# Hash attention and an MLP-Mixer block: second-level block products for all channel products, weight pieces on GpSimd, range loads on SyncE

## The chip, the core and the metric

One core of one Trainium2 chip runs the kernel. TensorE multiplies into PSUM, VectorE (DVE) and ScalarE (ACT) read PSUM and work in SBUF, GpSimd (POOL) does a few additions in SBUF and issues some DMAs, SyncE (SP) issues most DMAs. All engines run their instructions in order and wait for one another by semaphores. The metric is device time in microseconds; smaller is better.

## The reference

Attention over 4 batches of 8 heads, 768 positions, head size 64, where a query sees only the keys with the same 6-bit hash; then a Mixer block on the (4, 768, 512) result. All of it is float32.

```python
q_bits = (einsum('bhsd,dk->bhsk', q, proj) > 0)        # and k_bits
mask = q_bucket[:, :, :, None] == k_bucket[:, :, None, :]
attn = softmax(where(mask, q @ k.T / 8, -1e9));  x = attn @ v     # (4, 768, 512)
h = maximum(x.T @ w_tok1, 0) @ w_tok2                  # token mixing, 768 -> 256 -> 768
u = x + h.T
out = u + maximum(u @ w_ch1, 0) @ w_ch2                # channel mixing, 512 -> 1536 -> 512
```

## The kernel before

The program has three stages, one after the other: attention (0 to 310 us), token mixing (310 to 388 us), channel mixing (388 to 789 us). The change is in the third, the function `channels`. It works on columns of `XT`, the 512 channels by 3072 positions, in three ranges of 1024 positions (s = 0, 1, 2). In every range a first product (512 to 1536, with relu) fills the rows `R`, and a second product (1536 to 512) makes the output.

Both products are done as two-by-two block products with seven multiplications instead of eight (p1 to p7, with sums of blocks as operands, in the scheme of Strassen and Winograd). The sums of weights are made once: `SW1` and `SW2` on the first level. On a second level a product p1 to p7 can itself be split by seven; its left operands are then four more sums and three raw quarters of the weight, "pieces", which are made once during the first range and stored in DRAM (`hidden_passed` for the first product, `passed` for the second), and fetched again for every use.

- `hidden(0, t)`, t = 0 to 5, is the first range's first product: one level, seven products of two 512-column matmuls each. Between its own instructions VectorE makes pieces: `jobs` holds lists, and one list is run in the middle of a step and one at its end (lines 818 and 1341). `parts` (line 1046) makes four sums with VectorE and SyncE stores them, from a place that is shared (`seen`) or a free stretch of `area(1)`.
- `hidden_pair(s, t)`, three times in each later range: p2, p6, p3 and p4 are split by seven (`Smaller`, 256 columns), p1, p5 and p7 are whole (512 columns).
- `outputs(s)`, the second product in the order p1, p5, p7, p6, p3, p2, p4: p1 whole (`whole_product`, line 1137), the others split by seven (`product`, line 1151). In the first range p1 reads its weights from `WC2`, where they lie already. Before p5's turn and later, `fetch_left(g)` brings the seven blocks of the product after next into `area(g % 2)`.
- PSUM is used in four pairs of banks, which the products take in turn (`ring`).
- `look()` loads a range of q or k through GpSimd's queue and has ScalarE square it and compare it with a bound (two activations of 128x768, 32 times in all); a flag at the end chooses whether a careful version of the attention has to be run. The calls stand in the later ranges' pairs and in the second products of the first two ranges.

The order of everything is written out by hand: the Python code issues the instructions of all engines in one order, and each engine takes its own in that order. A DMA on SyncE's queue also waits for the DMA eight before it.

Helpers that record many operations have one line in the profile: every channel matmul is L779, copies from PSUM are L785, the piece sums are L1056 to L1059, and their stores L1067 to L1077.

Of the kernel before, what the change touches and what calls it, by code (L numbers as in the profile page):

```python
# [48 lines left out]
def kernel(  # L49
# [701 lines left out]
    def channels(pool, psum, SW1, second, TA, judge):  # L751

        KC, HC, QC = NCB // 2, NHT // 2, NHT // 4
        TB = pool.tile([P, 2, KC, TT], F32, name="TB", tag="TB", bufs=1)
        T = [TA[:, 0], TB[:, 0], TA[:, 1], TB[:, 1]]

        R = [pool.tile([P, 2, HC, TT // 2], F32, name=f"R{i}", tag=f"R{i}", bufs=1) for i in range(4)]
        q1 = pool.tile([P, KC, TT], F32, name="q1", tag="q1", bufs=1)
        last = B * S // (2 * TT) - 1

        def copies():
            return pool.tile([P, 2 * TT], F32, name="c", tag="c", bufs=3)


        ring = [0, 1, 2, 3]

        def bank_pair(i):
            return psum.tile([P, 2, TT], F32, name=f"b{i}", tag=f"b{i}", bufs=1)

        def blocks(n):  # L770

            now = ring[:n]
            ring[:] = ring[n:] + now
            return [bank_pair(i) for i in now]

        def accumulate(ps, left, right, ks, start=True, stop=True):
            ks = list(ks)
            for k in ks:
                nc.tensor.matmul(  # L779
                    ps, left(k), right(k), start=start and k == ks[0], stop=stop and k == ks[-1],  # L780
                    skip_group_check=True,
                )

        def copy(ps, c):
            nc.scalar.copy(c, ps)  # L785
            return c
# [3 lines left out]

        unfinished = []

        def end_rows():

            if unfinished:
                unfinished.pop()()

        def hidden(s, t):
# [6 lines left out]
            ps = [b[:, i] for b in blocks(2) for i in range(2)]  # L805
# [5 lines left out]
            p1 = copy(ps[0], c[0])  # L811
            p5 = copy(ps[2], c[1])
            accumulate(ps[0], lambda k: SW1[:, 0, k, low], lambda k: T[1][:, k], ks, False)
            p7 = copy(ps[3], c[2])
            end_rows()
            nc.vector.tensor_tensor(r[0], split(ps[1]), split(p1), op=ALU.add)
            nc.vector.tensor_scalar(r[0], r[0], 0.0, None, op0=ALU.max)
            for job in jobs.pop(0) if jobs else []:
                job()
            nc.gpsimd.tensor_tensor(p7, p5, p7, op=ALU.add)  # L820
            accumulate(ps[2], lambda k: SW1[:, 2, k, low], lambda k: XT[:, KC + k, sl[1]], ks, False)
            accumulate(ps[3], lambda k: WC1[:, KC + k, high], lambda k: T[3][:, k], ks, False)
            u = copy(ps[0], c[3])
            for k, a in [(3, p7), (1, ps[2]), (2, ps[3])]:
                nc.vector.tensor_tensor(r[k], split(a), split(u), op=ALU.add)
# [325 lines left out]
        def product(s, j, name, q, between, final=None):  # L1151
# [26 lines left out]
            if s < last:  # L1178
                look()
# [294 lines left out]
```

## Time and profile before

| | us |
|---|---|
| median of 3 runs | 796.18 (796.17 to 799.4) |
| the profiled execution | 795.77 |
| its span, first to last instruction | 794.0 |
| TensorE busy in the span | 786.4 |
| channel stage | 388 to 789 |
| `hidden(0, t)`, six steps | 388 to 460 |

A page of the profile is made from one execution. Its rows name engine, line and tile; "busy" is time in instructions, and an engine's idle time is put down to the engine or DMA that ended it. A window's row gives for each engine the busy time and the number of instructions in that stretch, then the granted TensorE clock (1.00 is full), the share of time that the 16 DMA engines were busy, and GB/s. "SPq" rows are SyncE's DMA issues.

### The profile page before, as it was taken

The page shows a single profiled execution, that of the slowest core. Times are in us where ns is not written, and L with a number is a line of the kernel's source. Part 1 is how long each engine was busy: PE and PEld are TensorE (multiplying, and loading weights), DVE is VectorE, ACT ScalarE, POOL GpSimd, SP SyncE. Part 2 cuts the span into 40 slices and gives each one's busy share as a digit, 9 for nine tenths or more (in the row PEclk, how much of TensorE's full clock was granted, in tenths as well). Part 3 has the DMA queues.
Part 4 walks back from the last instruction along what each step waited for, and adds up shares of the span by engine and source line. Part 5 has one row for each costly group of instructions (what it writes and reads, how often), then busy time and mean ns, then how long its engine had stood idle before and what let it go on. Part 6 is the DMA issues. An engine that isn't in the chain of part 4 may idle for free.

```text
span 794.0 us, 12166 instructions
## 1 busy us (share of the span) xinstructions
PE 786.4 (99%) x4661; PEld 464.9 (59%) x4661; DVE 659.7 (83%) x885; ACT 441.4 (56%) x706; POOL 53.5 (7%) x77
## 2 busy tenths in 40 slices
PE   8999999999999999999999999999999999999997
PEld 4444444444444444455544458876667886666886
DVE  5989898988987677999688788988769897778986
ACT  6688888888888886333323221327773335775111
POOL 1000000000000000011121010111110012000001
PEclk9999999999999999999999999999999999999999
DMA  4435353538352425796726994699754578730456
GB/s 163 163 123 163 123 163 123 163 122 246 143 178 87 154 47 166 215 281 173 175 60 228 334 356 145 185 294 283 218 148 139 217 204 195 218 109 1 148 176 159
DMA packets 90974, 138.67 MB, mean 175 GB/s; under 512 B 29656, under 2 KB 63392, under 8 KB 88608
## 3 DMA queue, kind: packets, MB, share of 16 engines
q1 hardware_dynamic: 82752, 112.86, 42.9%
q0 software_dynamic: 7728, 24.64, 14.0%
q8 instruction: 38, 0.62, 0.3%
q10 hardware_dynamic: 432, 0.34, 0.2%
q14 instruction: 24, 0.20, 0.1%
HBM read 97.21 MB, written 33.16 MB: 164 GB/s over the span
## 4 chain that ended last, share of the span: by engine, by line
PE 99%; DMA 1%; SPq 0%; DVE 0%; issue 0%
PE b L779 50%; PE sc L353 20%; PE acc L406 16%; PE t L652 5%; PE t L692 5%; PE sums L430 2%; PE hp L301 1%; DMA qk<-in_qk 1%; PE hw L325 0%; SPq L271 0%; DVE second L1202 0%; PE b L1319 0%; SPq L1469 0%
## 5 line engine op out<-in xcount | busy, mean ns | idle before, releaser
L360 ACT ACTIVATE e<-sc 128x768 f32<-128x768 f32 x192 | 154.1, 811 | 11.6 <-PE sc L353 11.2
L353 PE MATMUL sc<-qk 64*128 64x384 f32 x768 | 152.6, 483 | 0.0
L779 PE MATMUL b<-R,second 128*128 128x256 f32 (+1 forms) x612 | 150.9, 404 | 0.0
L779 PEld LDWEIGHTS b<-R,second 128*128 128x128 f32 x612 | 116.3, 190 | 31.6 <-issue 17.2
L785 ACT COPY c<-b 128x512 f32<-128x512 f32 (+1 forms) x78 | 37.4, 488 | 169.2 <-PE b L779 159.6
L406 PE MATMUL acc<-e,vn 128*32 128x384 f32 x1536 | 127.0, 486 | 0.0
L391 DVE TENSOR_TENSOR esd<-esd,e 128x768 f32<-128x768 f32 x96 | 92.0, 958 | 10.4 <-ACT e L360 0.5
L406 PEld LDWEIGHTS acc<-e,vn 128*32 128x32 f32 x1536 | 49.9, 110 | 73.9 <-issue 73.3
L353 PEld LDWEIGHTS sc<-qk 64*128 64x128 f32 x768 | 68.2, 187 | 40.8 <-issue 35.6
L779 PE MATMUL b<-XT,WC 128*128 128x256 f32 (+1 forms) x264 | 82.5, 456 | 0.0
L779 PEld LDWEIGHTS b<-XT,WC 128*128 128x128 f32 x264 | 50.2, 190 | 29.6 <-issue 25.1
L353 PE MATMUL sc<-bits 64*128 64x384 bf16 x384 | 62.5, 323 | 0.0
L387 DVE SCALAR_TENSOR_TENSOR esd<-e 128x768 f32<-128x768 f32 x32 | 30.6, 955 | 24.5 <-ACT e L360 24.5
L652 PE MATMUL t<-x,W 128*128 128x512 f32 x96 | 41.8, 593 | 0.0
L353 PEld LDWEIGHTS <-bits 64*128 64x128 bf16 x384 | 18.7, 94 | 33.0 <-issue 9.0
L712 POOL DMA_DIRECT2D XT<-second x8 | 9.9, 1232 | 386.0 <-DVE second L711 361.6
L451 ACT COPY rec<-rec 32x384 f32<-32x384 f32 x64 | 32.6, 510 | 5.0 <-DVE rec L445 4.2
L412 ACT ACTIVATE num<-acc,vsum 128x384 f32<-128x384 f32 x32 | 18.6, 581 | 29.8 <-PE acc L406 29.4
L779 PE MATMUL b<-XT,SW 128*128 128x256 f32 (+1 forms) x120 | 34.6, 422 | 0.0
L779 PE MATMUL b<-TA,WC 128*128 128x512 f32 x72 | 33.8, 592 | 0.0
L779 PE MATMUL b<-TA,SW 128*128 128x512 f32 x72 | 32.9, 592 | 0.0
L394 DVE TENSOR_TENSOR esd<-esd,e 128x768 f32<-128x768 f32 x32 | 30.5, 954 | 1.9
(217 smaller groups left out, 1129.3 us busy)
## 6 DMA issues: line engine op xcount, KB each, us to landing
second<-left SPq DMA_DIRECT2D x18, 1344.0 KB
raw<-in_moe_w_ch SPq DMA_DIRECT2D x16, 768.0 KB
qk<-in_qk SPq DMA_DIRECT2D x15, 768.0 KB
seen<-in_qk POOLq DMA_DIRECT2D x21, 384.0 KB, 3.8
WC<-hidden_left SPq DMA_DIRECT2D x15, 448.0 KB
vn<-in_v SPq DMA_DIRECT2D x16, 384.0 KB
vt<-in_vT SPq DMA_DIRECT2D x16, 384.0 KB
x<-bounced SPq DMA_DIRECT2D x4, 1536.0 KB
```

Source lines behind the costliest of these rows:

```text
L353: nc.tensor.matmul(sc[:, i, :HALF], t[rows, 1, P * c : P * c + P], t[rows, 0, qs], start=start, stop=not start,)
L360: nc.scalar.activation(e, sc[:, :, :HALF], ACT.Exp, scale=SCALE)
L387: nc.vector.scalar_tensor_tensor(self.d, es[0], NR * EPS, es[1], op0=ALU.add, op1=ALU.add,)
L391: nc.vector.tensor_tensor(self.d, self.d, e, op=ALU.add)
L394: nc.vector.tensor_tensor(self.d, self.d, self.es[-1], op=ALU.add)
L406: nc.tensor.matmul(acc[D * i + d : D * i + d + 32], vn[:, i, c, d : d + 32], e[:, i], start=(c == 0), stop=(c == NR - 1),)
L412: nc.scalar.activation(nums[self.n][:, self.half], acc, ACT.Identity, scale=-1.0, bias=vsum,)
L451: nc.scalar.copy(rec[other : other + 32, h], rec[at : at + 32, h])
L652: nc.tensor.matmul(ps, W1[:, r, P * j : P * j + P], x[:, r], start=(r == 0), stop=(r == NR - 1),)
L692: nc.tensor.matmul(ps[at], left, right, start=start, stop=True, skip_group_check=True,)
L779: nc.tensor.matmul(ps, left(k), right(k), start=start and k == ks[0], stop=stop and k == ks[-1], skip_group_check=True,)
L785: nc.scalar.copy(c, ps)
```

## The change

Six things change in `channels`:

1. All seven first products of the later ranges, and all seven second products of every range, are split by seven with 256 columns. One routine, `go(y)`, writes the order for both kinds: it interleaves the five multiplications of a product `y` with the last two of the product before it.
2. PSUM is cut into a tile per bank. A product takes two of six banks in turn, `a` and `c`, and a quarter of the last two banks, `b`. The first multiplication's result is copied by ScalarE from `a` to `b` inside PSUM, and further matmuls add to both ("seeded").
3. In the first product the sums over the seven names are run up name after name: VectorE adds the quarters 0 and 1 straight from PSUM, GpSimd the quarters 2 and 3 from SBUF.
4. The pieces of the first weight, now for seven names instead of four, are made by GpSimd, into rows of `R1` to `R3` that are not written yet; those of the second weight, seven instead of six, stay with VectorE. The order of the jobs changes. p1 of the second product no longer reads `WC2` in place: its blocks are stored and fetched like the others (`fetch_left(0)` ahead of the last `hidden` step).
5. `fetch_left` is cut in two, blocks 0 to 4 and the last two. Of the pieces for the next range's first products eight are kept instead of five; in the first range eight fetches are issued together in p2's `work`.
6. `look()` loads by SyncE's queue instead of GpSimd's, and is called in the gaps of second products only (up to three in each), after three loads at the start of `outputs(0)`.

The core of the diff:

```diff
-        ring = [0, 1, 2, 3]
-        def bank_pair(i):
-            return psum.tile([P, 2, TT], F32, name=f"b{i}", tag=f"b{i}", bufs=1)
+        def bank(i):
+            return psum.tile([P, TT], F32, name=f"b{i}", tag=f"b{i}", bufs=1)
...
+        def go(y, work=[], early=[]):
+
+            x, flow.before = flow.before, y
+            y.places()
+            y.mm(y.a, 4, 0)
+            copy(y.b, y.a)
+            y.mm(y.c, 1, 5)
+            y.first_done()
+            if x:
+                x.mm(x.a, 3, 3, False)
+                x.one()
+            run(early)
+            gap(y, 2 if y.patient else 1)
+            y.mm(y.a, 2, 6, False)
+            y.take(y.u, 2)
+            run(work)
+            y.mm(y.b, 5, 2, False)
+            y.second_done()
+            y.zero()
+            gap(y)
+            if x:
+                x.mm(x.c, 6, 7, False)
+                x.two()
+                x.end()
+            y.mm(y.a, 0, 4, False)
+            y.take(y.u5, 3)
+            y.three()
+            y.spent()
+            gap(y)
...
+        class Hidden(Product):
...
+            def head(self, ps, i):
+                if not self.add:
+                    copy(self.sum[0](i), ps)
+                for a, to in zip(self.add, self.sum):
+                    tt(to(i), ps, a(i))
...
+            def end(self):
+                for a, to in zip(self.add, self.sum):
+                    nc.gpsimd.tensor_tensor(
+                        to(slice(2, 4)), split(self.copies[:, 2 * N :]), a(slice(2, 4)), op=ALU.add,
+                    )
+                run(self.after)
+                fetch_hidden_left(self.h + 8)
...
+            plan = dict(
+                p1=([], [e]), p2=([e], [r0]), p6=([e], [u]), p5=([u], [v]), p3=([v], [r1]),
+                p7=([v, u], [r3, w]), p4=([w], [r2]),
+            )
...
-            def parts(w, store, other=False):
+            def parts(w, place, store, engine):
                 def job():
                     (a00, a01), (a10, a11) = weight_quarters(w)
...
+                    engine.tensor_tensor(new[1], a00, a10, op=ALU.subtract)
+                    engine.tensor_tensor(new[0], a10, a11, op=ALU.add)
+                    engine.tensor_tensor(new[2], new[0], a00, op=ALU.subtract)
+                    engine.tensor_tensor(new[3], a01, new[2], op=ALU.subtract)
+                    store(to, [a00, a01, a11])
...
+                return parts(first_weight(name), unwritten(i), store, nc.gpsimd)
...
             return [
-                [], sums, [whole("p1"), second_parts("p7")], *([second_parts(name)] for name in ("p6", "p3", "p5", "p2", "p4")),
-                *([hidden_parts(name)] for name in SMALLER),
+                [hidden_parts("p1", 1), hidden_parts("p2", 2)],
+                [*sums, hidden_parts("p6", 3)],
+                [second_parts("p7"), hidden_parts("p5", 1)],
+                [second_parts("p1", unwritten(0)), hidden_parts("p3", 2)],
+                [second_parts("p6"), hidden_parts("p7", 3)],
+                [second_parts("p3"), hidden_parts("p4", 1)],
+                [second_parts("p5")],
+                [second_parts("p4")],
+                [second_parts("p2")],
             ]
...
+        def fetch_left(g, n=slice(0, 7)):
 
             if g < 7 * (last + 1):
-                name = ORDER[g % 7]
-                n = (HC * 2 if name in WHOLE else 7 * QC) * P
-                nc.sync.dma_start(out=left_at(g)[:, :n], in_=passed[name])
+                sl = slice(QC * P * n.start, QC * P * n.stop)
+                nc.sync.dma_start(out=left_at(g)[:, sl], in_=passed[ORDER[g % 7]][:, sl])
...
+                if s == 0:
+                    work["p2"] += [lambda h=h: fetch_hidden_left(h) for h in range(8)]
...
-                nc.gpsimd.dma_start(out=t, in_=qk[pairs[n][0], pairs[n][1], :, i])
+                nc.sync.dma_start(out=t, in_=qk[pairs[n][0], pairs[n][1], :, i])
...
         for t in range(HC):
             if t == 1:
                 residual(0)
-            if t == 4 if judge else t == 0:
-                if not judge:
-                    fetch_left(0)
+            if t == HC - 2:
                 fetch_left(1)
-            hidden(0, t)
-            for job in jobs.pop(0) if jobs else []:
-                job()
+            if t == HC - 1:
+                fetch_left(0)
+                hidden(0, t, opening(0))
+                break
+            hidden(0, t, jobs.pop(0) if jobs else [])
+            run(jobs.pop(0) if jobs else [])
```

Two classes that `go` is called with are new. `Hidden` is a first product of the later ranges (one matmul for each of its multiplications), `Second` a second product (three matmuls each); `first_done` and `second_done` of `Second` make the operand sums that were made in `product`, `spent` and `end` issue the two parts of `fetch_left(g + 2)`. In `hidden` the addition into `r[3]` moves behind the other additions of the step.

## The prediction

> **What bounds the kernel now.** I read the page first, then the chain of waits, then the timelines of the engines in the stage that the change rebuilds (388 to 789 us). The page says that TensorE never rests:
>
> ```profile
> span 794.0 us, 12166 instructions
> PE 786.4 (99%) x4661; PEld 464.9 (59%) x4661; DVE 659.7 (83%) x885; ACT 441.4 (56%) x706; POOL 53.5 (7%) x77
> PEclk9999999999999999999999999999999999999999
> ```
>
> The chain that ended last is TensorE almost alone. Its pieces give the price of a pass (start, us, what; each f32 product of the code is two passes):
>
> ```profile
> 350.54 9.03 PE t L692 x28
> 359.57 10.30 PE t L652 x24
> 388.17 364.23 PE b L779 x1308
> 752.51 36.28 PE b L779 x168
> ```
>
> L652 passes are 512 columns wide: 10.30/24 = 0.429 us. The last 168 passes are 256 wide: 36.28/168 = 0.216 us. So a pass costs its columns, halves are not dearer, and the only gains left are fewer columns. Anything that makes TensorE wait is a loss, since today nothing does.
>
> The first range's `hidden` steps (t = 0 to 5, 28 passes or 12.07 us each, 388.1 to 460.5) share their time with the making and storing of weight pieces. There the DMA engines are already full (columns: window, us, busy time and count of each engine, granted clock, DMA share, GB/s):
>
> ```profile
> 437.80:446.00 8.20, 8.20 (x21) 3.65 (x20) 5.85 (x12) 3.05 (x6) 1.27 (x1) 1.00 1.00 337
> 446.00:456.00 10.00, 10.00 (x25) 4.50 (x24) 7.00 (x14) 1.67 (x4) 0.00 (x0) 1.00 1.01 328
> 456.00:466.00 10.00, 10.00 (x24) 4.38 (x24) 8.85 (x17) 3.13 (x6) 1.91 (x2) 1.00 0.94 367
> ```
>
> And VectorE and GpSimd hinder each other there. Two timelines of that stage, VectorE's and GpSimd's (start, us, engine, line):
>
> ```profile
> 407.93 1.76 DVE L746 TENSOR_TENSOR second<-second 128x1536 f32<-128x1536 f32 x1
> 409.72 2.70 DVE L747 TENSOR_TENSOR second<-second,second 128x1536 f32<-128x1536 f32 x1
> 420.64 1.52 DVE L1059 TENSOR_TENSOR seen<-second,seen 128x384 f32<-128x384 f32 x1
> 425.53 0.56 DVE L1056 TENSOR_TENSOR seen<-second 128x384 f32<-128x384 f32 x1 [2.31 <-DMA left<-seen]
> ```
>
> ```profile
> 408.24 2.57 POOL L820 TENSOR_TENSOR c<-c 128x512 f32<-128x512 f32 x1 [6.79 <-ACT c L785]
> 420.26 1.48 POOL L820 TENSOR_TENSOR c<-c 128x512 f32<-128x512 f32 x1 [9.45 <-ACT c L785]
> 456.31 1.27 POOL L820 TENSOR_TENSOR c<-c 128x512 f32<-128x512 f32 x1 [10.74 <-ACT c L785]
> ```
>
> At 456 GpSimd's add met no VectorE work and took 1.27 us. At 408 it met L746 and took 2.57; L747, queued behind it, took 2.70 instead of 1.76. At 420 L1059 took 1.52 instead of 0.56. So VectorE instructions with two SBUF inputs and GpSimd's adds run one after the other. The fourth row shows the other chain: the next piece waits 2.31 us until the store of the last one has left the shared place.
>
> **TensorE's gain.** In the two later ranges p1, p5 and p7 of the first product go from 4 products of 512 columns (8 passes, 3.43 us) to 7 of 256 (14 passes, 3.02 us): 0.41 us, times 3 names, 3 pairs, 2 ranges = 7.3 us. The second product's p1 goes from 24 passes of 512 (10.29 us) to 42 of 256 (9.07 us): 1.22 us, three times, 3.7 us. Sum 11.0 us. With no new wait the profiled execution (795.8 us, of which 794.0 are span) would become 784.8, the median 796.2 becomes 785.2.
>
> **The new wait before the second product.** Until now p1 took its weights from `WC2` in place. Now it needs its seven blocks by `fetch_left(0)`, which SyncE issues only after every piece of both weights was made and stored, since it overwrites the tile that p2's last blocks are stored from. p1 cannot start before that fetch lands; today it starts at 460.5. Two sums say when:
>
> By bytes: SyncE's queue carries 7 first and 7 second names of 1344 KB (1.376 MB) each, 19.3 MB, the residual of 4 times 512 KB, 2.1 MB, and both fetches, 2.75 MB: 24.1 MB. Before, up to the same point, it was less, and no fetch was awaited at 460. The first piece can leave when GpSimd has made four, about 405. At the 328 to 367 GB/s of the full windows that takes 66 to 74 us: 471 to 479, and about 1 to 2 us to land. A wait of 11 to 20 us.
>
> By engines: GpSimd gets 28 pieces of 384 columns. No row has one; by the 1.27 us of 512 columns one costs 0.95 (bounds: 0.56, VectorE's own, and 1.27). With five adds of 1.27 that is 33 us. VectorE's two-input work up to p2's pieces is 4 x 1.76 (sums), 28 x 0.56 (pieces), about 10 x 0.69 and 10 x 0.42: 34 us. If they alternate, 67 us from 399.7 end at 467, and waits for the shared place (2.3 us as in the row above, six of them, partly beside GpSimd's turn) take it to about 472. Then p2's blocks must be stored (six DMAs, 1.376 MB, 4.1 us at 337 GB/s, and issue and landing 2.5) and p1's fetched (4.1 and 1.5): about 484. If VectorE and GpSimd did not hinder each other this sum falls below the other one, and bytes decide.
>
> I take 484, a wait of 23 us, with 11 and 30 as ends. On GpSimd the add for `p7` of the next t is queued behind up to twelve pieces, on VectorE `r[3]` waits for that add and the next pieces stand behind `r[3]`; on SyncE the first range loads and the next fetch stand behind `fetch_left(0)`. Within the 23 us TensorE also waits earlier (t = 2 on: a copy needs a buffer that GpSimd's add still reads), which is the same time, not more.
>
> **The second products of the first range.** 20 range loads (393 KB) now fall in these seven products, on SyncE's queue, in order with the weights. DMA time by rows: a fetch of 1.376 MB at 138 GB/s and share 0.39 (730 to 740 us) is 3.9 us, six of them 23; range loads at that rate 1.1 each, 22; eight accumulating output stores at 162 GB/s and share 0.89 (388 to 392) 2.9 each, 23; eight pieces for the next range at 315 GB/s and share 1.10 (530 to 536) 1.6 each, 13. That is 81 us in 63.5 us of TensorE. What is not needed at once slides into the next stage. But p4's blocks 3 and 6 and three range loads are queued behind the eight pieces, and ScalarE, waiting for a range, holds up copies that free banks. Ends: 0 (all of it slides) and 17.5 (nothing does). I take 4, nearer to nothing, because the stage after has room (shares about 0.5 to 0.9).
>
> The Trainium skill ("DMA: Bandwidth & Descriptors", Queues, rings and completion order) says that each DMA engine takes turns between the queues that have work. That speaks against the move of the range loads: on GpSimd's queue they had a turn of their own, on SyncE's they stand behind the weights. In this trace GpSimd's range loads landed 3.8 to 6.1 us after issue; no row here has one on SyncE's queue. By the rule alone a load behind the eight pieces would wait their whole 13 us (an estimate), where ScalarE comes for it a product, 9 us, later: the sum would be 4 us longer.
>
> **Parts near nothing.** The seed: a ScalarE copy from PSUM to PSUM, not in the trace; nearest is 0.37 us for 128x256 from PSUM to SBUF. TensorE does two other products between (0.86 us in the first product, 2.6 in the second). Cover is gone if a relu of 0.58 stands ahead: 0.1 us, up to 36 times, 3.6 us at most; taken as 0. GpSimd's adds in the first product, 1.27 us once or twice per 3.02 us, meet VectorE instructions that read PSUM, which no row shows hindered: 0. A tile per bank frees banks earlier, but TensorE waits for none: 0, no gain. The end has one VectorE add fewer after the last pass: -0.4 us.
>
> Sum: 796.2 - 11.0 + 23 + 4 = 812 us.
>
> **Rivals.**
> Covers hold (faster): stores run at the best rate seen for 4 us (409 GB/s, 456 to 460), so 24.1 MB take 59 us, p1 waits about 5 us, and nothing else shows: 785 to 792. It decides if p1's fetch lands before 471.5, when the wait eats the 11 us. Against it: the full windows above, in which less was stored. 0.16.
> Only bytes decide: wait 11 to 20, later stage 0 to 4: 796 to 808. For it: pieces on GpSimd leave VectorE 16 instructions fewer. 0.24.
> Both chains, my forecast: wait 20 to 30, later 0 to 8: 805 to 822. 0.46.
> The first range's second products become DMA-bound as well: 10 to 17 more on 23: 818 to 832. 0.14.
>
> Half a per cent, 4 us, is about what can be told from no change. Below 792.2 lies the first rival, 0.16; between 792.2 and 800.2 a third of the second, 0.08; above it 0.76. The range 791 to 828 leaves out most of the first rival and the top of the last.
>
> **What would show it.** Right: 14 passes per 3.02 us in all first products of the later ranges; rows of 384 columns on VectorE in the `hidden` steps stretched to about 1.5 us beside GpSimd; TensorE idle for 20 us or more before the first 256-wide pass, released by the DMA that fills `second`. Wrong: p1 starting by 465, GpSimd's pieces ending by 435, or a DMA rate over 400 GB/s throughout. If TensorE stands in the second products for ScalarE, the third term is larger.

## The result and the profile after

The changed kernel takes 877.63 us (median of 4 runs, 874.0 to 882.8) against 797.79 us of the kernel before: 1.100 times as long, interval 1.094 to 1.107. The prediction was 812, range 791 to 828: the direction was right, the size far off. The profiled execution took 874.0 us, its span 872.2.

The head of the changed kernel's page:

```profile
span 872.2 us, 12935 instructions
PE 795.1 (91%) x4823; PEld 499.1 (57%) x4823; DVE 646.1 (74%) x936; ACT 460.0 (53%) x830; POOL 141.1 (16%) x126
PEclk9999999999999999999998799789999996999999
```

TensorE, which never rested, is idle for 9% of the span. Two things more: it is busy 8.7 us longer than before although its passes are 11 us shorter, and its clock is no longer full in five of the 40 slices. TensorE's timeline gives the places (start, us, instruction; in brackets the idle time before it and what ended that):

```profile
485.24 2.93 PE L777 MATMUL b<-R,second 128*128 128x256 f32 x6 [14.06 <-DMA second<-left]
561.90 2.93 PE L777 MATMUL b<-R,second 128*128 128x256 f32 x6 [12.74 <-ACT c L783]
568.65 1.22 PE L777 MATMUL b<-WC 128*128 128x256 f32 x2 [3.81 <-ACT b L783]
...
734.88 1.22 PE L777 MATMUL b<-WC 128*128 128x256 f32 x2 [15.06 <-ACT c L783]
...
852.05 1.56 PE L777 MATMUL b<-second,second 128*128 128x256 f32 x6 [2.37 <-DVE second L787]
854.91 9.45 PE L777 MATMUL b<-R,second 128*128 128x256 f32 x42 [1.29 <-DVE c L787]
```

The first row is the wait that was predicted, at 485 instead of 484. The others were not predicted, or only as a few microseconds. The six passes in the first row hold TensorE for 2.72 us, to the next start at 487.96, where six take 1.30 at full speed: each of the long waits (3.8 us and more here) is followed by slow passes.

To compare runs I use a **loss** for each stage: the time from its first pass to the first pass of the next stage, less its passes. H0 is `hidden` of the first range (72.1 us, as before), O0, O1, O2 are the second products (7 x 9.07 = 63.5), H1 and H2 the later first products (21 x 3.02 = 63.4). Where `go` interleaves, the last multiplications of a stage stand behind the first ones of the next: 2.6 us move from O0 and O1 into the stage behind, 0.9 from H1 and H2. The passes sum to 389.4 us against the measured 400.8 of the kernel before. Losses, in us, and the time of each experiment's one run:

| run | H0 | O0 | H1 | O1 | H2 | O2 | time |
|---|---|---|---|---|---|---|---|
| changed kernel | 23.2 | 2.0 | 26.8 | 4.2 | 20.1 | 8.8 | 874.0 |
| e1 pieces on VectorE | 17.1 | 2.7 | 31.2 | 4.2 | 19.8 | 9.0 | 871.0 |
| e9 residual later | 19.1 | 2.0 | 23.9 | 4.2 | 18.5 | 9.4 | 864.7 |
| e15 both of these | 13.5 | 1.5 | 26.6 | 4.2 | 19.8 | 9.4 | 864.7 |
| e7 p1 in place | 8.1 | 11.2 | 26.0 | 4.2 | 19.1 | 9.1 | 866.4 |
| e2 range loads on GpSimd | 24.5 | 3.1 | 30.4 | 5.0 | 20.3 | 9.5 | 880.0 |
| e3 fetches spread | 23.0 | 4.5 | 25.1 | 4.2 | 19.8 | 9.6 | 872.6 |
| e10 no late range loads | 22.7 | 1.8 | 27.2 | 4.5 | 21.6 | 9.1 | 875.5 |
| e13 half the range check | 23.3 | 1.5 | 26.7 | 4.2 | 21.9 | 9.1 | 875.0 |
| e4 adds on VectorE | 23.0 | 2.8 | 23.1 | 3.2 | 12.4 | 8.8 | 861.2 |
| e5 four stores | 22.8 | 8.7 | 15.4 | 8.8 | 6.2 | 10.3 | 858.7 |
| e6 = e4 + e5 | 22.9 | 8.0 | 17.2 | 8.0 | 7.0 | 10.4 | 857.1 |
| e14 = e6 + half the range check | 23.0 | 5.2 | 5.6 | 8.0 | 5.6 | 10.4 | 843.7 |
| e8 = e6 + e7 | 8.9 | 9.7 | 18.4 | 6.3 | 5.6 | 10.4 | 844.6 |
| e11 all remedies | 2.2 | 13.1 | 4.5 | 8.8 | 7.3 | 12.3 | 834.4 |

For the changed kernel: 795.8 (profiled before) - 11.4 (passes) + 85.1 (losses) + 2.6 (from the last pass to the end: 7.8 instead of 5.2) + 1.9 (the channel stage began later, at 389.9) = 874.0. Such a start varies from 387.4 to 390.3 over the runs, and four runs of the changed kernel spread over 9 us, so the losses, not the times, carry the small differences. Each of these is one run too: in the runs whose edit leaves a stage alone H0 lies between 22.7 and 24.5 and H2 between 18.5 and 21.9, and differences of that size say nothing. The kernel before took 795.7 to 798.5 beside the experiments.

**What stands behind the loss in H2.** The change doubles the accumulating stores of the output: each of the sums that were added up in SBUF before is now sent out by itself. From the lists of DMA issues, the kernel before and then the changed one (count, size, median us to landing):

```profile
out<-second POOLq DMA_DIRECT2D x10, 512.0 KB, 8.4
```

```profile
out<-second POOLq DMA_DIRECT2D x17, 512.0 KB, 8.3
out<-q POOLq DMA_DIRECT2D x4, 512.0 KB, 8.2
```

21 stores instead of 10. GpSimd's timeline of the changed kernel at the end of the second range:

```profile
700.55 1.22 POOL L1296 DMA_DIRECT2D out<-second  x1 [5.04 <-issue]
706.89 1.21 POOL L1296 DMA_DIRECT2D out<-second  x1 [5.11 <-issue]
716.79 1.22 POOL L1296 DMA_DIRECT2D out<-second  x1 [8.69 <-ACT c L783]
725.01 1.21 POOL L1296 DMA_DIRECT2D out<-q  x1 [6.99 <-issue]
731.39 1.22 POOL L1296 DMA_DIRECT2D out<-second  x1 [5.17 <-issue]
732.15 1.76 POOL L1035 TENSOR_TENSOR R<-c,second 128x512 f32<-128x512 f32 x1
```

A store is busy for 1.2 us, but the next starts 6.3 to 9.9 us after it, in three of the four gaps for nothing that the profile names ("issue"). The landings show what it is: the stores at 694.30, 700.55, 706.89, 716.79 and 725.01 land after 5.9, 6.0, 9.6, 7.9 and 6.1 us, and the next store starts 0.3 us after each landing. In all 17 traces of this case no accumulating DMA on this queue starts before the one ahead of it has landed (0.26 us after it at the least). Other instructions don't wait so: the add at 732.15 starts 0.76 us behind the last store, and in the kernel before a plain range load does the same:

```profile
539.26 1.24 POOL L1222 DMA_DIRECT2D out<-second  x1 [10.78 <-DVE XT L848]
540.03 1.07 POOL L1307 DMA_DIRECT2D looked<-in_qk  x1
```

So a store does not fill the queue by itself; it is the next store that waits, and all that stands behind that one. Four are still to come when the third range begins at 706, and the first `L1035` add of that stage stands behind all of them. ScalarE waits for this add with its relu, and for a range load one range earlier:

```profile
559.69 0.84 ACT L1388 ACTIVATE looked<-looked 128x768 f32<-128x768 f32 x1 [13.57 <-DMA looked<-in_qk]
...
733.94 0.63 ACT L793 ACTIVATE R<-R 128x512 f32<-128x512 f32 x1 [15.74 <-POOL R L1035]
```

Behind both stand copies that free TensorE's banks. The range load comes late because SyncE, whose DMAs each wait for the eighth before them, was held up by the fetches ahead of it:

```profile
538.93 12.10 SPq L975 DMA_DIRECT2D SW<-hidden_left  x5
551.45 3.72 SPq L1399 DMA_DIRECT2D looked<-in_qk  x1
```

**Short waits in H1 and H2.** Some 4 us of the loss in each of these two stages have another cause. Where nothing long stands in the way, seven first products (98 passes, 7 x 3.02 = 21.1 us) take 22.56 us, at full clock and with the DMA engines nearly idle; the kernel before took 22.39 us for the same seven (windows of the changed kernel and of the kernel before, columns as in the prediction):

```profile
766.29:788.85 22.56, 22.13 (x100) 18.20 (x99) 12.53 (x30) 11.23 (x30) 8.85 (x8) 1.00 0.14 41
```

```profile
524.80:547.19 22.39, 22.39 (x82) 15.20 (x81) 17.95 (x29) 11.49 (x20) 4.74 (x6) 1.00 0.98 265
```

The 1.4 us are three waits of 0.24 us and one of 0.69 in every group of seven. Each stands where ScalarE does a relu (L793) right ahead of the copy that TensorE needs. No run here moves these relus, so that this cause is read from the rows alone. Two of the waits in the changed kernel, ScalarE's rows and then TensorE's:

```profile
618.06 0.63 ACT L793 ACTIVATE R<-R 128x512 f32<-128x512 f32 x1
618.59 0.38 ACT L783 COPY b<-b 128x256 f32<-128x256 f32 x1
620.07 0.63 ACT L793 ACTIVATE R<-R 128x512 f32<-128x512 f32 x1 [1.10 <-POOL R L1035]
620.60 0.35 ACT L783 COPY c<-b 128x256 f32<-128x256 f32 x1
```

```profile
619.02 0.70 PE L777 MATMUL b<-WC,SW 128*128 128x256 f32 x2
621.01 0.70 PE L777 MATMUL b<-WC,SW 128*128 128x256 f32 x2 [0.43 <-ACT c L783]
```

### The profile page after: what moved, and what is told of

It reads as the page before. It is cut to its first block, busy times and chain, and to the rows that moved or that the text cites. A ratio compares the mean times of both kernels' runs of the same rounds, so it can differ in the third digit from the quotient of the medians.

```text
span 872.2 us, 12935 instructions
## 1 busy us (share of the span) xinstructions
PE 795.1 (91%) x4823; PEld 499.1 (57%) x4823; DVE 646.1 (74%) x936; ACT 460.0 (53%) x830; POOL 141.1 (16%) x126
## 3 DMA queue, kind: packets, MB, share of 16 engines
q0 software_dynamic: 8160, 17.83, 12.4%
## 5 line engine op out<-in xcount | busy, mean ns | idle before, releaser
L777 PE MATMUL b<-R,second 128*128 128x256 f32 x594 | 140.2, 388 | 29.7 <-DMA second<-left 14.1
L783 ACT COPY c<-b 128x256 f32<-128x256 f32 (+1 forms) x146 | 58.5, 405 | 130.5 <-PE b L777 107.0
L391 DVE TENSOR_TENSOR esd<-esd,e 128x768 f32<-128x768 f32 x96 | 92.0, 958 | 10.4 <-ACT e L360 0.5
L793 ACT ACTIVATE R<-R 128x512 f32<-128x512 f32 x48 | 29.7, 630 | 59.8 <-POOL R L1035 28.5
L777 PE MATMUL b<-XT,SW 128*128 128x256 f32 (+1 forms) x208 | 60.7, 405 | 0.0
L777 PE MATMUL b<-XT,WC 128*128 128x256 f32 (+1 forms) x164 | 54.9, 453 | 0.0
L787 DVE TENSOR_TENSOR R<-R 128x768 f32<-128x768 f32 x45 | 44.5, 1000 | 6.5 <-PE b L777 5.9
L787 DVE TENSOR_TENSOR c<-b,c 128x256 f32<-128x256 f32 x72 | 29.7, 421 | 26.2 <-ACT c L783 21.7
L777 PEld LDWEIGHTS b<-XT,SW 128*128 128x128 f32 x208 | 39.0, 190 | 11.7 <-issue 5.5
L1035 POOL TENSOR_TENSOR R<-c,second 128x512 f32<-128x512 f32 x24 | 31.4, 1309 | 65.7 <-DVE c L787 65.4
```

Source lines behind the costliest of these rows:

```text
L391: nc.vector.tensor_tensor(self.d, self.d, e, op=ALU.add)
L777: nc.tensor.matmul(ps, left(k), right(k), start=start and k == ks[0], stop=k == ks[-1], skip_group_check=True,)
L783: nc.scalar.copy(to, ps)
L787: nc.vector.tensor_tensor(to, a, b, op=op)
L793: return lambda: nc.scalar.activation(a, a, ACT.Relu)
L1035: nc.gpsimd.tensor_tensor(to(slice(2, 4)), split(self.copies[:, 2 * N :]), a(slice(2, 4)), op=ALU.add,)
```

## The experiments

### The wait before the second product (H0)

**e1**

```diff
-                return parts(first_weight(name), unwritten(i), store, nc.gpsimd)
+                return parts(first_weight(name), unwritten(i), store, nc.vector)
```

> The first weight's pieces are made by VectorE instead of GpSimd; nothing else differs from the changed kernel. Question: what holds the second product's p1 until 485 us. Theory 'DMA': the 24.1 MB of stores and fetches decide, GpSimd's pieces were over by 443.7 and the DMA engines ran at share 1.0 and 351 to 385 GB/s from 428 to 460, so the first 256-wide pass of the second product starts at 480 to 488 again and the time stays within 4 us of 874. Rival 'engines' (the sum that the prediction took): VectorE and GpSimd hold each other up, without that p1 starts at 470 to 478 and 8 to 15 us are saved. Third: VectorE's own queue gets 28 pieces of about 0.56 us (16 us) more and becomes later itself, p1 at 490 or more.

Measured: p1 at 477.2, 89.2 us after the first layer's first pass instead of 95.3. So the engines hold each other up by 6 us, less than the rival said (477.2 lies in its stretch only because the stage began 1.9 us earlier in this run), and DMA alone is not it either. H1 lost 4.4 us more in this one run.

**e9**

```diff
             if t == 1:
-                residual(0)
...
             if t == HC - 1:
                 fetch_left(0)
+                residual(0)
```

> The four stores of the residual of the first range (2.1 MB), which SyncE issues in the changed kernel after the first step, are issued after the fetch for p1; nothing else differs. If DMA bytes alone hold p1 until 485, it starts 5 to 6 us earlier relative to the first pass of the first layer (2.1 MB at 351 to 385 GB/s; 95.3 us from there in the changed kernel, so 89 to 91). If the chain of VectorE, GpSimd and the shared place decides, it starts where it did (95 to 96). With both, in turn, something between, 91 to 94. The whole time gains no more than that, and gives back some of it where the 2.1 MB then run.

Measured: 91.2 us instead of 95.3, in the stretch named for "both, in turn".

**e15**, both edits.

> First weight's pieces on VectorE and the residual's four stores after the fetch for p1, each of which alone took 6.1 and 4.1 us from the first layer's first range (95.3 us; 72.1 without a wait). If the two are links of one chain in turn (first engines, then bytes), they add: 84 to 86 us. If bytes alone are left once the engines are out of the way, the residual's 2.1 MB give their full 6 us: 82 to 84. If they cover each other: 88 to 89.

Measured: 85.6 us. They add up: first a chain of engines, then bytes. The windows of the changed kernel show the two parts (window, us, busy of PE, PEld, DVE, ACT, POOL, clock, DMA share, GB/s):

```profile
410.00:420.00 10.00, 10.00 (x25) 4.41 (x24) 9.90 (x7) 2.44 (x5) 9.76 (x6) 1.00 0.40 152
430.00:440.00 10.00, 10.00 (x24) 4.39 (x24) 9.39 (x11) 1.17 (x2) 9.75 (x8) 1.00 1.05 379
450.00:460.00 10.00, 5.59 (x13) 2.20 (x12) 4.20 (x9) 0.59 (x1) 1.27 (x1) 1.00 1.04 379
```

At 410 VectorE and GpSimd are full and the DMA engines wait for them; from 430 on the DMA engines are full, and at 450 VectorE is not.

**e7**

```diff
+            if s == 0 and judge:
+                for i in range(KC):
+                    ps = flow.bank()
+                    accumulate(ps, lambda k: second["WC2"][:, k, P * i : P * i + P], lambda k: R[0][:, :, k], range(HC))
...
+                    copy(q1[:, i], ps)
...
+                fetch_left(2)
```

> In the first range alone the second product's p1 takes its weights from WC2 in place, 24 passes of 512 columns (10.3 us instead of 9.1), as the kernel before does; its fetch there is left out, the rest is the changed kernel. Theory 'two separate waits': the wait before the second product (24.7 us and 2 to 3 of slower clock) goes, 1.2 comes back, 850 us. Rival 'one backlog': what is left out is 1.4 MB of some 24; the stores and loads that were worked off in these 25 us now lie beside the second products, and ScalarE and TensorE wait there or at the head of the next stage instead: of the 25 us at least 12 return, 861 to 875 in all. I hold the rival for the likelier, since the DMA engines ran at share 1.0 from 428 to 470 and from 508 to 570.

Measured: 866.4 us, within the rival's stretch. The long wait is gone, but of the 25.2 us lost in H0 and O0 only 5.9 are gained, with p1's 1.2 us of longer passes already taken out: 8.1 us remain in H0, mostly waits of 1.5 to 2.8 us for copies and rows (e11, with pieces on VectorE, has 2.2), and O0 loses 11.2 where it lost 2.0. The stores and loads that were worked off during the wait now lie beside the second products: TensorE waits 5.53 us for weight blocks at 491.77.

### The second range's start (O0 and H1)

**e2**, the range loads back on GpSimd's queue.

```diff
-                nc.sync.dma_start(out=t, in_=qk[pairs[n][0], pairs[n][1], :, i])
+                nc.gpsimd.dma_start(out=t, in_=qk[pairs[n][0], pairs[n][1], :, i])
```

> The range loads go back to GpSimd's queue. Question: the first stage of the second range lasts 92.0 us (548.1 to 640.2) instead of 63.5. Theory 'queue': its waits of 13.6 us of ScalarE for 'looked' and 4.6 for 'seen', which hold up the copies that free banks, come from the range loads' place behind the eight weight fetches on SyncE's queue; on GpSimd's queue they land before they are wanted and the stage takes 68 to 78 us, 14 to 24 less. But GpSimd's queue then has 20 loads more ahead of its adds, so its adds may cost up to 5 back. Rival 'bytes': the DMA engines have 81 us of work for 63.5 us of TensorE there, whichever queue it stands in: the stage stays above 85 us.

Measured: O0 and H1 lose 33.5 instead of 28.8, and the second range's first stage takes 95.6 us, above 85, as the rival said. Yet it is again a place in a queue: ScalarE now waited 20.0 us for the load at 555.86, which stands 0.71 us behind an output store on GpSimd's queue, and that store had to wait for the landing of the one before.

**e3**

```diff
-                    work["p2"] += [lambda h=h: fetch_hidden_left(h) for h in range(8)]
+                    for j, name in enumerate(ORDER[:6]):
+                        work[name] += [lambda h=h: fetch_hidden_left(h) for h in ([0, 1] if j == 0 else [6, 7] if j == 5 else [j + 1])]
```

> The eight weight fetches for the second range, which were all issued within the second product p2, are spread over p1 to p2 (two, one, one, one, one, two), in the same queue; the bytes are the same. Theory 'queue': no range load then stands behind eight fetches; ScalarE's wait of 13.6 us and TensorE's of 12.7 us at 560 go, the stage of the second range takes 66 to 75 us instead of 92.0, 17 to 26 less in the whole. Rival 'bytes': the waits only move forward, into the second products p5 to p3 of the first range, and the time from 485 to 640 stays within 6 us of the changed kernel's 155.

Measured: as the rival said. O0 and H1 lose 29.6, and from 482.6 to 638.3 it is 155.7 us. The 12.7 us wait became one of 5.3 us for a copy and one of 9.8 us behind GpSimd's add.

**e10**

```diff
-            elif flow.looks and y.patient:
+            elif flow.looks and y.patient and y.g not in (5, 6):
```

> In the first range's p2 and p4 no range load is issued or taken up; these few come in the second range's products instead. All else as in the changed kernel. Theory: ScalarE's wait for 'looked' (13.6 us at 560), with TensorE's 12.7 us behind it, is the wait for one range load behind eight weight fetches; here there is no such load, so that wait goes, but what was queued with it stays: p4's last two blocks (384 KB) stand behind the same eight fetches, and TensorE then waits 4 to 8 us for them ('DMA second<-left'): the time from the first pass of the second product (485) to that of the second range's outputs (642) falls from 157 to 145 to 151. Rival: the DMA engines decide, not the order: the wait for p4's blocks is as long as the one for ScalarE, 155 to 158 as before.

Measured: the wait for a range load is gone, TensorE waits 7.8 us for p4's blocks as expected ('DMA second<-left', at 555.9), but the stage is not shorter: 11.9 us behind GpSimd's add follow at 582.7. O0 and H1 lose 29.0, and from 484.4 to 639.5 it is 155.1 us: the theory's sign, and the rival's number.

**e13**, no range load in the first range after the first three; half of the check is left out.

```diff
-            elif flow.looks and y.patient:
+            elif flow.looks and y.patient and y.g > 6:
...
-        unseen = [(n, i) for n in range(len(pairs)) for i in range(2)] if judge else []
+        unseen = [(n, i) for n in range(len(pairs)) for i in range(2)][:16] if judge else []
```

> Left out: half of the range check, 16 of 32 loads, namely those that stand in the first range's second products after the first three (some 18 of 393 KB, 7 MB there); the second range keeps its 13 or so. All else as in the changed kernel. In the changed kernel the loss over passes is 2.0 us in the first range's second products and 26.8 in the second range's first products. Theory 'bytes': 7 MB at 330 GB/s are 21 us of full DMA engines; without them what is left fits, the two losses together fall from 28.8 to 5 to 12. Rival 'GpSimd's store queue': eight stores, 6.2 to 10 us apart, still reach 30 us into the next stage, GpSimd's adds stand behind them, and the two losses stay at 18 to 27, with ScalarE waiting for GpSimd's add (R<-...L1035) in the place of the range load, as in the third range.

Measured: 28.2 instead of 28.8, although 20 loads (7.9 MB) are gone from this stretch; four of them now come a range later. TensorE's timeline, and ScalarE's:

```profile
551.77 2.90 PE L777 MATMUL b<-R,second 128*128 128x256 f32 x6 [5.16 <-DMA second<-left]
580.04 1.22 PE L777 MATMUL b<-WC,SW 128*128 128x256 f32 x2 [12.29 <-ACT c L783]
```

```profile
579.10 0.63 ACT L793 ACTIVATE R<-R 128x512 f32<-128x512 f32 x1 [12.97 <-POOL R L1035]
```

The rival's sign is there, and its 18 to 27 us were still too few: with the range loads away, GpSimd's add behind the stores ends the wait, as in H2, 34.5 us after the stage's start, where the add's last wait ended 37.3 us after it in the changed kernel.

### GpSimd's stores and adds (H1 and H2)

**e4**

```diff
-                    nc.gpsimd.tensor_tensor(
+                    nc.vector.tensor_tensor(
                         to(slice(2, 4)), split(self.copies[:, 2 * N :]), a(slice(2, 4)), op=ALU.add,
```

> The adds that end a product of the first layer go from GpSimd to VectorE. Theory 'queue': on GpSimd they stand behind output stores whose issue takes 5 to 7 us each, so that ScalarE waited 15.7 us for one of them and TensorE 15.1 us behind it at 734; without that the stage of the third range takes 63 to 68 us instead of 85.3, that of the second range 2 to 6 less than 92.0, in all 19 to 28 us less. Rival 'DMA': the output stores and weight fetches are late by themselves, TensorE waits then for a DMA in the same place, and less than 6 us are saved. Against both: VectorE gets up to 36 adds of 256 to 512 columns (0.4 to 0.7 us, 14 to 25 us in two stages of 63.5) and could become late: then its waits show on ScalarE and TensorE as DVE.

Measured: H2 loses 12.4 instead of 20.1, H1 23.1 instead of 26.8; 12.8 us in the whole, between the theories. VectorE does not become late by its adds. It waits for the stores themselves, which still read the places that the stage writes its sums to:

```profile
729.17 0.42 DVE L787 TENSOR_TENSOR second<-b,second 128x256 f32<-128x256 f32 x1 [7.50 <-DMA out<-second]
```

**e5**, four stores per range. The sums are made in SBUF, p2 and p4 add in place, and the places are renamed so that the one stored last is needed last.

```diff
-            e, u, v, w = map(place, (3, 0, 1, 2))
+            e, u, v, w = map(place, (3, 2, 1, 0))
...
-            sums = [add(q7, q7, q6), add(q5, q5, q6)]
-            sums += [store(q5, 0, 1), *([store(q7, 1, 0), store(q7, 1, 1)] if more else [store(q6, 1, 1)])]
+            sums = [add(q7, q7, q6), add(q6, q6, q5), add(q5, q5, q7), store(q5, 1, 1)]
...
-                final = None
+                final = True if name in ("p2", "p4") else None
```

> Each range's output goes out in 4 accumulating stores instead of 8 (2 instead of 5 in the last range, whose DMA for the residual becomes an add): the quarters are summed on VectorE first, two adds of 1024 columns (1.22 us) more per range, and p2 and p4 add in place, 8 copies per range moving from ScalarE to VectorE. Theory 'GpSimd's issue': in the changed kernel stores that stand one behind the other on GpSimd start 6.2 to 6.4 us apart (725.01 and 731.39; 851.54, 857.82 and 864.00), whatever the DMA engines do, so six stores from the middle of a range's second products on take 37 us and reach 25 us into the next stage, where GpSimd's adds stand behind them and VectorE waits for places that they still read. With 4 stores the third range's first stage falls from 85.3 to 64 to 70 us, the second range's from 92.0 to 76 to 86 (the range loads' wait stays), the end loses 4 to 8: 834 to 850 in all. Rival 'the adds': GpSimd's adds are late by themselves, beside VectorE; then the third range's stage stays above 80.

Measured: in H2 ScalarE waits 1.1 us at most for GpSimd's add, and TensorE behind it 0.43; H2 loses 6.2 instead of 20.1, H1 15.4 instead of 26.8. The stores start up to 11.5 us apart beside other DMA work, not 6.2 to 6.4 "whatever the DMA engines do". The whole is 858.7, above the stretch that I gave: the sums make VectorE late (waits of 3.0 us in O0 and 2.6 in O1, with slow passes behind both), so that O0 and O1 lose 8.7 and 8.8 instead of 2.0 and 4.2, and the end gains only 1.3 in all.

**e6**, e4 and e5 together.

> Four stores per range, and the adds that end a first product on VectorE. If the stores are the cause of both waits in the third range's first stage (GpSimd's adds behind them, VectorE's wait for places that they read), this stage is within 2 us of 63.5 now, and the whole is 2 to 8 us below the kernel with four stores alone. Rival 'VectorE': 17 us more of adds there make VectorE late, and this is no better than four stores alone.

Measured: 857.1; H2 loses 7.0, not under 2, and the whole is only 1.6 us less, which is the rival's number. With H2 at 12.4 by e4 alone, 6.2 by e5 alone and 7.0 by both, the adds' place no longer matters once the stores are few: the two remedies remove one cause. Of what stays, some 4 us are the short waits.

**e14**, e6 and e13 together.

> Left out: the same half of the range check, on top of four stores per range and VectorE's adds at the end of a first product. Both theories expect most of the two losses (25.2 us with the four stores and VectorE's adds) to go: to 8 to 13, about the 15.0 that the same two stages lose one range later, where there are few range loads. If they stay above 18, neither bytes of range loads nor stores are the cause, and the eight weight fetches themselves are.

Measured: O0 and H1 lose 10.8, within 8 to 13. So H1 had two chains side by side, each about as long as the other: range loads and blocks behind the weight fetches on SyncE's queue, and the adds behind the stores on GpSimd's. Away with the first alone (e13): 0.6 us. With the second alone (e6): 3.6. With both: 18.0. The 3.6 are net of 6.0 us that the sums on VectorE cost in O0; by H1 alone it is 0.1, 9.6 and 21.2, still far more together than one by one. Whether the bytes of the range loads or their place in the queue make the first chain is not shown: e13 and e14 take away both.

### All together, and the clock

**e8**, e6 and e7.

> The three edits together: four stores per range, the adds on VectorE, p1 of the first range in place. If the three causes are separate their gains add up: the kernel with the first two, less 24 us, about 805 to 815. If there is one backlog of DMA work in the first range, fewer stores (2 MB of the output, each read and written) shrink it too, and waits of 10 to 25 us stay between 500 and 590, released by DMA or by ScalarE's range loads: 815 to 835.

Measured: 844.6, above both stretches: p1 in place gains 12.6 us here.

**e11**: e1, e4, e7, e5 with two of its sums on GpSimd, no range load in p2 and p4 of the first range (e10), and the eight fetches from p5 to p4.

> All remedies in one kernel: first weight's pieces, and the adds that end a first product, on VectorE; four accumulating stores per range, two of their sums on GpSimd itself; p1 of the first range in place; the eight fetches one or two to a product from p5 to p4; no range load in p2 and p4 of the first range. From 844.6 us of the three remedies before: about 6 less by the pieces (waits of 1.5, 2.1 and 2.8 us at 444 to 458), 8 to 12 less at 548 to 560 (6.7 and 4.1 us of waits and the slower clock after them), 4 to 7 less by VectorE's waits of 2.3 to 3.8 us at the sums: 818 to 828. If the DMA engines simply have too much to do between 420 and 570, the waits at 548 return as single waits for weight blocks in p7 to p3, and it stays above 832. Below the kernel before (796) it does not get by either theory.

Measured: 834.4, above 832 as the second theory said, but without its sign: no wait for weight blocks is longer than 0.6 us (at 513). H0 has nearly no loss (2.2), and of the 4.5 in H1 most are the short waits, since seven first products still take 22.38 us. What is left elsewhere are waits of 1 to 3 us for VectorE's sums, and what follows them, which neither theory had. TensorE's timeline at the opening of the second range's second product, and windows of the same place (columns as above; the clock is the third number from the right):

```profile
613.23 2.31 PE L777 MATMUL b<-q,second 128*128 128x256 f32 x6 [2.16 <-DVE q L787]
615.33 2.41 PE L777 MATMUL b<-R,second 128*128 128x256 f32 x6
```

```profile
612.00:614.00 2.00, 0.77 (x3) 0.72 (x4) 1.97 (x4) 0.00 (x0) 0.00 (x0) 0.96 0.00 0
614.00:616.00 2.00, 2.00 (x6) 1.59 (x5) 2.00 (x4) 0.37 (x1) 0.00 (x0) 0.50 0.00 0
616.00:618.00 2.00, 2.00 (x7) 1.64 (x7) 2.00 (x4) 0.22 (x2) 0.00 (x0) 0.69 0.00 0
618.00:620.00 2.00, 2.00 (x11) 1.76 (x10) 1.97 (x3) 1.97 (x5) 0.00 (x0) 1.00 0.00 0
```

A wait of 2.2 us, and then about 3.4 us at half clock (0.2 + 2.0 + 1.2 from the three clocks below 1), so that twelve passes from 613.23 take 4.35 us to 617.58 instead of 2.59.

**e12** asks whether the wait alone does this, in the kernel before.

```diff
+            for _ in range({1: 7, 2: 11}.get(t, 0)):
+                copy(ps[0], c[3])
             p1 = copy(ps[0], c[0])
```

> The kernel before, with two waits put into it where nothing else is short: ScalarE copies one PSUM bank 7 times more in the first layer's second step and 11 times more in its third, ahead of the copy that frees that bank for TensorE; the extra copies go to a buffer that is overwritten later. A copy takes about 0.52 us and there are 2.65 us of cover, so TensorE waits 1.0 to 1.5 us in the second step (about 407) and 3.0 to 3.7 us in the third (about 420). Question: does a wait cost more than itself? Theory 'clock': after a wait of over 2 us TensorE's granted clock is 0.50 for some 3 us (in the kernel with all remedies a wait of 2.16 us at 613 was followed by six passes in 2.31 and six in 2.41 us instead of 1.3), after one of 1.8 us or less it is not: so after the first wait passes keep 0.43 us each, after the second 5 to 8 of them take 0.86, and the third step costs 2 to 3 us more than its wait; in all 5.5 to 8.5 us over the kernel before if nothing else covers them. Rival: the lower clock comes with something else that those places share (the change from one stage to the next, full DMA engines); here, with DMA share 0.5 to 0.8, both steps cost their waits alone, 4 to 5 us.

Measured, on TensorE's timeline:

```profile
408.93 1.98 PE L779 MATMUL b<-TB,SW 128*128 128x512 f32 x4 [1.43 <-ACT c L785]
...
425.11 2.94 PE L779 MATMUL b<-TB,SW 128*128 128x512 f32 x4 [3.90 <-ACT c L785]
427.84 2.66 PE L779 MATMUL b<-XT,SW 128*128 128x512 f32 x4
430.34 1.88 PE L779 MATMUL b<-TB,WC 128*128 128x512 f32 x4
```

After 1.4 us the next group starts 1.82 us later (1.72 without a wait); after 3.9 us the next two start 2.73 and 2.50 us later: 1.8 us more than the wait. In all 803.5 against 795.7, and 7.8 us of span, of which the starts show 7.4: 1.6 and 4.1 by the waits (the groups ahead start at 405.62 and 419.33) and 1.8 by the clock. The clock follows the wait, with no change of stage near it.

How long must a wait be? In the changed kernel 1.79 us at 645, 2.13 at 452 and 2.37 at 852 left the clock at 1.00, 2.91 at 461 and all longer ones did not; in e11 2.16 us was enough, in e6 1.98 (706.86), while in e4 3.29 (838.49) was not. The Trainium skill ("TensorE: Matmul & The Clock Gate", Part 1) tells of a freely running window of about 3.4 us: an idle window halves the clock, a busy one restores it. The 3.4 us at half clock agree, and so does the grid: in the changed kernel the granted clock falls at 461.87, 475.52, 554.03 and 724.70, whole multiples of 3.413 us apart. Such a window would explain why waits of like length end differently. That only gaps over 3.4 us do harm, as its rule has it, the waits at 461 and 613 contradict.

No version reached the kernel before; the best, e11, is 38 us behind it.

## Why the prediction was wrong

**TensorE's gain** (11.0 us) was right for the passes (0.216 us each at full clock) and arrived in the second products, 9.07 us for each that did not wait. In the first products it did not arrive: seven of them take 22.56 us where the sum needs 21.1, and 22.39 before, so that the 7.3 us counted there are eaten. The condition stands in the prediction, a relu ahead of the seed, "0.1 us ... taken as 0"; it measured 0.24 us three times and 0.69 once in every seven, 8.5 us in six such groups if all are like the four quiet ones.

**The new wait before the second product** was right in place, cause and size: 484 said, 485.2 measured, first the engines' alternation, then bytes (e1, e9, e15). Inside it two errors cancel, which is luck: the engines were to alternate until 467 with some 5 us of waits for the shared place; GpSimd's last piece began at 442.41, and VectorE then waited 4.46, 3.95, 0.60 and 1.21 us for stores to leave that place while the DMA engines were full. What it left out is that this wait was time in which the DMA engines worked off what would otherwise stand in the way later (e7).

**The second products of the first range** is the step that failed: 4 us with ends 0 and 17.5, measured 28.8 over O0 and H1. Three things in it were wrong. The eight output stores were priced by the DMA time of their bytes, 2.9 us each, where each holds up the next on GpSimd's queue until it has landed, 6.4 to 11.5 us from start to start in the first range. The kernel before had the spacing in its rows: its accumulating DMAs at 385.68, 392.31 and 398.94 start 6.63 us apart. "The stage after has room" was said of the DMA engines, but that stage needs right at its start what slid into it: the weight blocks, the adds, the places that the stores read. And the sentence on SyncE's queue named the right wait (p4's blocks and a range load behind eight fetches) and then took almost nothing for it. The rule on DMA queues that was weighed there pointed the right way, and its 4 us were as much too small; that GpSimd's queue would have helped the range loads is refuted by e2, where they stand behind the stores, so that no run here tests the turns themselves. The 3.8 to 6.1 us given there are the medians of two kinds of range loads; single ones landed after 3.3 to 8.0 us.

**"GpSimd's adds in the first product: 0"** failed. The adds' own time was looked at, not what stands ahead of them on their queue; nor was it noticed that the change doubles those stores. This is most of the 20.1 us of H2 (13.9 go with four stores, e5), which no term and no rival held; some 4 are the short waits.

**"The end: -0.4 us"**: the last stage loses 8.8 us and the stretch behind the last pass 2.6 us more. About 4.2 of the 8.8 are lost at the stage's start, as in O1, by waits for sums on VectorE (1.79, 0.67 and 0.79 us). The rest comes at its end, by the same stores: the residual's accumulating DMA started at 840.27, right after a store had landed, VectorE waited 3.80 us for it before p4, and TensorE 2.37 and 1.29 us behind VectorE.

**Not in the sum at all**: slow passes behind a long wait, 1.7, 2.0, 4.4 and 1.7 us in four stretches of the changed kernel (from 461, 485, 562 and 735), some 10 us in all.

The rival that held both chains had the right mechanism for H0; the last rival (10 to 17 more for the first range's second products) was nearest, and its upper end of 832 us still 46 us short.

## What to carry to other kernels

When a change adds or moves DMAs, go through each queue they are issued from in order, with the spacing that two such issues have in the trace, and ask what compute instruction stands behind them; bytes over bandwidth gave only a lower bound here. A term that is "taken as 0" though its condition occurs in every step is to be multiplied out first: 0.24 us here, several times in each group, were more than the gain that they stood beside. A wait with two causes of about equal length showed only one of them in the profile: removing that one changed the name of the wait and nothing else, so take them away together before calling either harmless. And a kernel whose TensorE never waits has no slack that later stages could take up: what "slides" arrives at the next stage's first instruction.

## What the runs showed of the hardware

Accumulating DMAs on GpSimd's queue run one after the other: the next starts 0.3 us after the last has landed, for 512 KB at best 6.2 us from start to start (851.54, 857.82 and 864.00 at the changed kernel's end) and up to 11.5 beside other DMA work (554.69 and 566.14). Plain range loads of 384 KB on the same queue do not wait like this: in the kernel before two stand 0.96 us apart (540.03 and 540.99), right behind a store that lands only at 545.3. What orders the accumulating ones is not settled; the profile calls the wait "issue".

TensorE's clock can fall to 0.50 after as little as 2.0 us without work (e6, 706.86) and need not after 3.3 us (e4, 838.49). Where it fell behind a single short wait it stayed there for some 3.4 us, so that the wait cost about 1.8 us more than itself (e11, e12).

A piece of 384 columns took GpSimd 1.0 to 1.5 us beside short VectorE work and 2.4 to 2.5 beside VectorE's 1536-column sums (407 to 415), where 0.95 was estimated.
